# Attention and gated feed-forward on one core: the low parts of split q and k made on GpSimd, half of q split three steps sooner, and q of the last pairs loaded and rotated sooner

## The chip, the cores and the metric

The kernel runs on one core of a Trainium2 chip, as one program with five engines that run side by side: TensorE (PE in the rows; PEld is its weight load), VectorE (DVE), ScalarE (ACT), GpSimd (POOL) and SyncE (SP, which here only issues DMAs). Each engine works through its own instructions in the order in which they were written, and waits on semaphores for the others. The metric is the device time of one execution in microseconds (us), lower is better.

## What is computed

```python
def rotate(x):                       # rotary embedding, x1 and x2 are halves of the head
    return concat([x1 * cos - x2 * sin, x1 * sin + x2 * cos])
q_rot, k_rot = rotate(q), rotate(k)  # q, k, v: 4 batches x 8 heads x 576 tokens x 64
scores = q_rot @ k_rot.T / sqrt(64)
attn = softmax(scores)
x = (attn @ v)                       # heads put side by side: 4 x 576 x 512
h = relu(x @ w_in)                   # 512 -> 1024
c = conv over 3 neighbouring tokens of h, weights conv_w
out = (h * sigmoid(c)) @ w_out       # 1024 -> 512
```

All arrays are float32.

## The kernel before, in words

Two heads are treated together, which gives 16 pairs, numbered 0 to 15. A pair takes five steps, so pair p owns steps 5p to 5p+4; below they are called step 0 to step 4 of the pair. In each step one block of 128 query rows (64 in step 4, both heads at once) meets all 576 keys of its head. A step runs through these stations: the scores on TensorE into the PSUM tile `sp` (`emit_S`), the negated row maximum `negm` on VectorE (L292), the exponential on ScalarE into `st` (L296), and one step later the transposition of `st` on TensorE (L397) into PSUM tiles `tp`, which ScalarE copies to `pt` (L221). In step 0 of the next pair the product with v runs (L477), into PSUM tiles `pm`. From step 26 on, TensorE fills the rest of each step with the feed-forward part: first matmul units (L546, 24 matmuls each, whose results VectorE convolves at L565 and L567, and gates at L576) and halves of the second matmul (L658, whose two partial sums ScalarE and VectorE put together in `oh`, L672 and L673).

For speed, pairs 11 to 15 (`SPLITS = 11`) use split operands: a float32 x is written as hi + lo, where hi is x rounded by a copy to the type fp32r and lo = x - hi. The scores are then three products: KH with QH, KH with the low part of q, the low part of k with QH (L339; L333 for the last 64 rows, whose q lies in `QD`). The high parts QH, KH and QD are made by ScalarE (L370, L377, L386), the low parts `qL`, `kL` and half of QD by VectorE (L366, L375, L384), all of them in step 4 of the pair before (QD's low part in step 0 of the pair itself).

The rotated q and k come from the raw loads `rq` and `rk` (four DMAs each, issued by SP at L152, one buffer each). GpSimd multiplies them by a table (L192, six instructions for a tile) and adds the halves (L195, three instructions). VectorE turns the sum into `QT` and `KT` (L257, L260). GpSimd also makes the low parts of the feed-forward activations: `xT` and `xm` at L502, `gm` and `gb` at L585, each after ScalarE has made the high part.

What runs when is set by a table: `at(n, rank, fn)` puts a piece of work into step n, and within a step the pieces are written in the order of their ranks. Every engine then keeps that order. So a rank decides behind which other work of its engine an instruction stands. The tiles of the pool `p2` have two buffers for each tag: `QT` and `qL` share the tag `qT`, `KT` and `kL` the tag `kT`.

For the pair p the plan of before is: load q and k in step 5p-10 (rank 19.6), rotate q in step 5p-8 and k in step 5p-7, transpose both in step 5p-5 (rank 0.45), split in step 5p-1.

## Time and profile before

| What | Value |
|---|---|
| time, median of 3 runs | 465.98 us (465.52 to 466.04) |
| profiled execution, its own time | 466.01 us |
| profiled execution, span from the first to the last instruction | 464.2 us |
| granted TensorE clock over the span | 1.0 of full speed (the 2.4 GHz level) |
| busy: TensorE, VectorE, ScalarE, GpSimd | 448.6, 361.1, 333.4, 276.1 us |

The span is the profiler's; 1.8 us of the execution's own time lie around it. A busy engine is one that executes an instruction. Matmuls are pipelined, so that the busy time of TensorE is no measure of how close it is to its peak; what counts below is when TensorE stands still, and for whom.

### The profile page before, as it was taken

How to read it: one execution, taken by the hardware profiler on the slowest of the kernel's cores; microseconds unless marked ns; L12 is line 12 of the kernel's file. 1: busy time of each engine (PE TensorE's matmuls, PEld its weight loads, DVE VectorE, ACT ScalarE, POOL GpSimd, SP SyncE). 2: the span in 40 equal slices, each digit the busy share in tenths (PEclk: the TensorE clock that was granted, in tenths of full speed). 3: DMA queues.
4: the chain of work that ended last, by engine and by line, in shares of the span. 5: the costliest groups of instructions: out<-in, count | busy, mean ns of one | idle time of the engine just before them, and what ended most of it. 6: DMA issues, size and time to landing. Idle time of an engine off the chain costs nothing.

```text
span 464.2 us, 12800 instructions
## 1 busy us (share of the span) xinstructions
PE 448.6 (97%) x4843; PEld 353.5 (76%) x4843; DVE 361.1 (78%) x670; ACT 333.4 (72%) x960; POOL 276.1 (59%) x403
## 2 busy tenths in 40 slices
PE   8799999999999999999999989899999999999997
PEld 7366666666656767788887969798897978999886
DVE  6788999969998988687697997977976648468911
ACT  2899999979897878778696868778796844245500
POOL 1765555767998896979687593929530234144510
PEclk9999999999999999999999999999999999999999
DMA  9978784743463316142252517143110000100011
GB/s 226 240 173 222 197 222 111 203 105 79 117 129 75 68 42 137 38 104 63 55 101 61 120 38 140 39 97 81 29 51 34 18 28 0 47 23 24 0 70 45
DMA packets 103633, 42.36 MB, mean 91 GB/s; under 512 B 94524, under 2 KB 97876, under 8 KB 103572
## 3 DMA queue, kind: packets, MB, share of 16 engines
q1 hardware_dynamic: 103120, 41.20, 36.9%
q8 instruction: 38, 0.62, 0.6%
q10 hardware_dynamic: 452, 0.35, 0.2%
q14 instruction: 23, 0.19, 0.1%
HBM read 36.74 MB, written 4.79 MB: 89 GB/s over the span
## 4 chain that ended last, share of the span: by engine, by line
PE 71%; ACT 14%; DVE 11%; POOL 2%; issue 1%; DVEq 0%; POOLq 0%; ACTq 0%
PE mt L638 11%; PE pm L477 10%; PE pm L658 8%; PE pm L546 8%; PE mt L546 7%; PE tp L397 6%; PE sp L284 6%; ACT st L296 5%; ACT pt L221 4%; PE pm L527 4%; PE sp L339 3%; PE sp L477 3%; DVE c L567 3%; DVE negm L292 2%; DVE c L576 1%
## 5 line engine op out<-in xcount | busy, mean ns | idle before, releaser
L292 DVE TENSOR_REDUCE negm<-sp 128x1 f32<-128x576 f32 x144 | 102.6, 749 | 19.5 <-PE sp L339 6.9
L296 ACT ACTIVATE st<-sp,negm 128x576 f32<-128x576 f32 x128 | 94.2, 745 | 19.6 <-DVE negm L292 19.0
L221 ACT ACTIVATE pt<-tp 128x512 f32<-128x512 f32 (+3 forms) x176 | 84.7, 535 | 5.6 <-PE tp L397 5.0
L567 DVE SCALAR_TENSOR_TENSOR c<-rr,cw,c 128x288 f32<-128x288 f32 x128 | 80.5, 629 | 4.2
L585 POOL TENSOR_TENSOR gm<-c,gm 128x288 fp32r<-128x288 f32 (+4 forms) x72 | 46.4, 650 | 48.9 <-ACT gm L584 47.5
L284 PE MATMUL sp<-kT,qT 64*128 64x288 f32 (+3 forms) x352 | 64.3, 470 | 0.3 <-ACT kT L221 0.3
L397 PEld LDWEIGHTS tp<-idf,st 64*128 64x128 f32 x1024 | 40.4, 138 | 15.0 <-ACT st L296 6.7
L477 PE MATMUL pm<-pt,vm 128*64 128x290 f32 x368 | 49.7, 411 | 0.4 <-ACT pt L221 0.4
L658 PE MATMUL pm<-wouth,gm 64*128 64x256 f32 x512 | 49.8, 284 | 0.0
L397 PE MATMUL tp<-idf,st 64*128 64x64 f32 x1024 | 45.9, 226 | 3.5 <-ACT st L296 3.2
L192 POOL TENSOR_TENSOR rq<-rq,tabt 128x192 f32<-128x192 f32 x60 | 39.9, 697 | 13.7 <-DMA rq<-q 13.7
L576 DVE SCALAR_TENSOR_TENSOR c<-c,rr 128x288 f32<-128x288 f32 x64 | 38.3, 619 | 10.3 <-ACT c L573 10.3
L192 POOL TENSOR_TENSOR rk<-rk,tabt 128x192 f32<-128x192 f32 x60 | 41.0, 716 | 2.5 <-DVE negm L292 2.5
L658 PEld LDWEIGHTS pm<-wouth,gm 64*128 64x128 f32 x512 | 42.2, 186 | 0.0
L565 DVE TENSOR_SCALAR c<-rr,cw 128x288 f32<-128x288 f32 x56 | 25.2, 450 | 19.3 <-ACT rr L557 18.3
L284 PEld LDWEIGHTS sp<-kT,qT 64*128 64x128 f32 (+1 forms) x352 | 27.8, 173 | 15.4 <-issue 6.0
L477 PEld LDWEIGHTS pm<-pt,vm 128*64 128x64 f32 x368 | 25.6, 136 | 17.7 <-ACT pt L221 1.0
L502 POOL TENSOR_TENSOR xT<-xn,xT 128x290 fp32r<-128x290 f32 x18 | 16.0, 893 | 36.3 <-ACT xT L498 36.3
L658 PE MATMUL pm<-woutl,gm 64*128 64x256 f32 x256 | 37.6, 278 | 0.0
L573 ACT ACTIVATE c<-c 128x288 f32<-128x288 f32 x64 | 28.6, 447 | 12.1 <-DVE c L567 12.1
L546 PE MATMUL pm<-xT,wh 128*128 128x290 f32 x176 | 37.0, 302 | 0.0
L527 PE MATMUL pm<-xr,wr 128*64 128x290 f32 x256 | 33.9, 412 | 0.0
(161 smaller groups left out, 1064.5 us busy)
## 6 DMA issues: line engine op xcount, KB each, us to landing
rq<-q SPq DMA_DIRECT2D x60, 144.0 KB
rk<-k SPq DMA_DIRECT2D x60, 144.0 KB
w<-moe_w_in SPq DMA_DIRECT2D x8, 512.0 KB
vm<-v SPq DMA_DIRECT2D x32, 128.0 KB
rb<-rd SPq DMA_DIRECT2D x16, 144.0 KB
out<-oh SPq DMA_DIRECT2D x18, 128.0 KB
rb<-rd SPq DMA_DIRECT2D x16, 128.0 KB
w<-moe_w_out SPq DMA_DIRECT2D x4, 512.0 KB
```

Source lines behind the costliest of these rows:

```text
L192: nc.gpsimd.tensor_tensor(out=y, in0=y, in1=tabt[:, a:a + 3], op=ALU.mult)
L221: nc.scalar.activation(out=out, in_=in_, func=AF.Copy, scale=1.0 if sc is None else sc)
L284: nc.tensor.matmul(out=out, lhsT=qt[64 * h:64 * h + 64, c], rhs=kt[64 * h:64 * h + 64, a:a + n], start=True, stop=True)
L292: reds.setdefault((p, s), []).append(lambda: nc.vector.tensor_reduce(out=nm, in_=sc, axis=AX.XY if len(sc.shape) == 3 else AX.X, op=ALU.ma ...
L296: lambda: nc.scalar.activation(out=dst, in_=sc, func=AF.Exp, bias=nm, scale=1.0, accum_out=sm)
L397: nc.tensor.transpose(ps[r][:, 64 * k:64 * k + 64], x[i], idf[i, i])
L477: nc.tensor.matmul(out=xp[64 * h:64 * h + 64, :], lhsT=vmain[p][:, h, i, :] if i < 4 else vrem[p % 2][:, h, :], rhs=pt[:, 2 * i + h if i < ...
L527: nc.tensor.matmul(out=ps[a:a + 64], lhsT=w[:, a:a + 64], rhs=x, start=start, stop=stop)
L546: nc.tensor.matmul(out=ps[:, 0:XW], lhsT=w, rhs=x_at(xs, e), start=(i == 0), stop=(i == n - 1))
L567: nc.vector.scalar_tensor_tensor(out=c, in0=r[:, j + e:j + e + HS], scalar=cw[:, 8 * e + f:8 * e + f + 1], in1=c, op0=ALU.mult, op1=ALU.add,)
L638: nc.tensor.matmul(out=ops[tt][:, 0:width], lhsT=g_tile(tt, f, e), rhs=w[:, f, cols], start=(f == 0 and i == 0), stop=(f == NF - 1 and i = ...
L658: nc.tensor.matmul(out=ps[r][:, 0:256], lhsT=g_tile(tt, f, e)[rows], rhs=w[rows, f, cols], start=(f == 0 and i == 0), stop=(f == NF - 1 an ...
```

## The change

The low parts of q, k and QD move from VectorE to GpSimd (`lower`). They are kept in one tile each for all pairs (`late["qT"]`, `late["kT"]`, named `qTl` and `kTl`), which hold one of the two buffers of their tag for good. Rows 0 to 255 of q of pairs 12 to 15 are split in step 5p-4 in place of step 5p-1. In step 5p-1 KH comes first (rank 0.05) and the second half of QH and QD come behind the exponential (ranks 1.55 and 1.57); the low part of QD moves from step 5p to step 5p-1. For pairs 12 to 15 the load of q is issued right behind the transposition that frees its buffer (rank 0.46 in place of 19.6), its rotation moves from step 5p-8 to 5p-9, the multiplications of k from step 5p-7 to 5p-8, and the additions of k to step 5p-6 (rank 1.53).

```diff
-    def rope(p, part):
+    def rope(p, part, mult=True, add=True):
         x = raw[p, part]
-        for a in range(0, 18, 3):
+        for a in range(0, 18 * mult, 3):
             y = x[:, a:a + 3]
             nc.gpsimd.tensor_tensor(out=y, in0=y, in1=tabt[:, a:a + 3], op=ALU.mult)
-        for a in range(0, 18, 6):
+        for a in range(0, 18 * add, 6):
...
-            qs = (QD[:, 0], QD[:, 1]) if whole else (late["QH"][:, c], QL[p][:, c])
-            for i, (w, x) in enumerate(((qs[0], KH), (qs[1], KH), (qs[0], KL[p]))):
+            qs = (QD[:, 0], QD[:, 1]) if whole else (late["QH"][:, c], late["qT"][:, c])
+            for i, (w, x) in enumerate(((qs[0], KH), (qs[1], KH), (qs[0], late["kT"]))):
...
-    def split_q(p, low):
-        x = QT[p][:, 0:512]
+    def lower(tag, width, a, b, x, hi):
+        if tag not in late:
+            late[tag] = p2.tile([128, width], F32R, tag=tag, name=tag + "l")
+        nc.gpsimd.tensor_tensor(out=late[tag][:, a:b], in0=x, in1=hi.bitcast(F32), op=ALU.subtract)
+
+    def split_q(p, low, a, b):
+        x = QT[p][:, a:b]
         if low:
-            QL[p] = p2.tile([128, S], F32R, tag="qT", name="qL")
-            nc.vector.tensor_tensor(out=QL[p][:, 0:512], in0=x, in1=late["QH"].bitcast(F32), op=ALU.subtract)
+            lower("qT", S, a, b, x, late["QH"][:, a:b])
             return
...
-        nc.scalar.activation(out=late["QH"], in_=x, func=AF.Copy)
+        nc.scalar.activation(out=late["QH"][:, a:b], in_=x, func=AF.Copy)
 
     def split_k(p, low):
         if low:
-            KL[p] = p2.tile([128, S + 64], F32R, tag="kT", name="kL")
-            nc.vector.tensor_tensor(out=KL[p], in0=KT[p], in1=KH.bitcast(F32), op=ALU.subtract)
+            lower("kT", S + 64, 0, S + 64, KT[p], KH)
...
-                nc.vector.tensor_tensor(out=lo, in0=x, in1=hi.bitcast(F32), op=ALU.subtract)
+                nc.gpsimd.tensor_tensor(out=lo, in0=x, in1=hi.bitcast(F32), op=ALU.subtract)
...
-                        at(max(n - 10, WIDE) if early else n - 9 + 2 * i, 19.6 if early else 16 if p == 2 else 0.36, lambda p=p, part=part: load(p, part))
+                        at(max(n - 10, WIDE) if early else n - 9 + 2 * i, 0.46 if p > SPLITS and not i else 19.6 if early else 16 if p == 2 else 0.36, lambda p=p, part=part: load(p, part))
...
+                    elif p > SPLITS:
+                        at(n - 9 + i, 18, lambda p=p, part=part, i=i: rope(p, part, add=not i))
+                        if i:
+                            at(n - 6, 1.53, lambda p=p, part=part: rope(p, part, mult=False))
...
-                    for m, rank, fn, low in (
-                        (n - 1, 0.05, split_q, 0), (n - 1, 0.22, split_q, 1), (n - 1, 1.4, split_k, 0), (n - 1, 1.45, split_k, 1),
-                        (n - 1, 1.42, split_rest, 0), (n, 0.42, split_rest, 1),
+                    lead = (n - 4, 1.55) if p > SPLITS else (n - 1, 0.04)
+                    for (m, rank), fn in (
+                        (lead, lambda p, low: split_q(p, low, 0, 256)),
+                        ((n - 1, 0.05), split_k),
+                        ((n - 1, 1.55), lambda p, low: split_q(p, low, 256, 512)),
+                        ((n - 1, 1.57), split_rest),
                     ):
-                        at(m, rank, lambda fn=fn, p=p, low=low: fn(p, low))
+                        for low in range(2):
+                            at(m, 18.5 if low and m < n - 1 else rank + 0.05 * low, lambda fn=fn, p=p, low=low: fn(p, low))
```

On TensorE the order stays as it was. On GpSimd the stretch from the activations `gm` in step 1 of pair 12 to the next pair's `gm` in step 1 stood like this before (q and k are those of pair 14, which is rotated two pairs ahead).

```order
L502 TENSOR_TENSOR xT<-xn,xT 128x290
L192 TENSOR_TENSOR rq<-rq,tabt 128x192 x6
L195 TENSOR_TENSOR rq<-rq 128x6x32 x3
L502 TENSOR_TENSOR xT<-xn,xT 128x290
L192 TENSOR_TENSOR rk<-rk,tabt 128x192 x6
L195 TENSOR_TENSOR rk<-rk 128x6x32 x3
L585 TENSOR_TENSOR gm<-c,gm 128x288 x4
```

In the changed kernel the same stretch stands like this.

```order
L192 TENSOR_TENSOR rq<-rq,tabt 128x192 x6
L195 TENSOR_TENSOR rq<-rq 128x6x32 x3
L363 TENSOR_TENSOR qTl<-qT,QH 128x256
L503 TENSOR_TENSOR xT<-xn,xT 128x290
L192 TENSOR_TENSOR rk<-rk,tabt 128x192 x6
L503 TENSOR_TENSOR xT<-xn,xT 128x290
L363 TENSOR_TENSOR kTl<-kT,KH 128x640
L586 TENSOR_TENSOR gm<-c,gm 128x288 x2
L195 TENSOR_TENSOR rk<-rk 128x6x32 x3
L363 TENSOR_TENSOR qTl<-qT,QH 128x256
L385 TENSOR_TENSOR QD<-qT,QD 64x64 x2
L586 TENSOR_TENSOR gm<-c,gm 128x288 x2
```

The low part of k of pair 13 now stands behind both rotations' multiplications and both `xT`, and the additions of k, the second half of q and QD stand between the two groups of `gm`.

On VectorE, from step 4 of pair 12 to the transposition in step 0 of pair 13, the order before was this.

```order
L292 TENSOR_REDUCE negm<-sp 128x1
L366 TENSOR_TENSOR qL<-qT,QH 128x512
L565 TENSOR_SCALAR c<-rr_1576,cw 128x288
L567 SCALAR_TENSOR_TENSOR c<-rr_1576,cw,c 128x288 x2
L375 TENSOR_TENSOR kL<-kT,KH 128x640
L673 TENSOR_TENSOR oh<-oh,pm 128x256
L292 TENSOR_REDUCE negm<-sp 128x1 x2
L576 SCALAR_TENSOR_TENSOR c<-c,rr_1575 128x288
L576 SCALAR_TENSOR_TENSOR c<-c,rr_1576 128x288
L384 TENSOR_TENSOR QD<-qT,QD 64x64 x2
L257 STREAM_TRANSPOSE qT<-rq 128x576
```

In the changed kernel it is this.

```order
L292 TENSOR_REDUCE negm<-sp 128x1
L566 TENSOR_SCALAR c<-rr_1576,cw 128x288
L568 SCALAR_TENSOR_TENSOR c<-rr_1576,cw,c 128x288 x2
L674 TENSOR_TENSOR oh<-oh,pm 128x256
L292 TENSOR_REDUCE negm<-sp 128x1 x2
L577 SCALAR_TENSOR_TENSOR c<-c,rr_1575 128x288
L577 SCALAR_TENSOR_TENSOR c<-c,rr_1576 128x288
L257 STREAM_TRANSPOSE qT<-rq 128x576
```

Three kinds of subtraction have left VectorE; nothing else changed place there. The transposition of q (L257) writes the buffer that the low part of QD (L385, now on GpSimd) reads last.

On SP, the DMAs of step 0 of a pair stood like this before.

```order
L451 DMA rd<-rt 9x32 x4
L457 DMA rb<-rd 64x576
L458 DMA rb<-rd 64x512
L459 DMA rb<-rd 64x64
L152 DMA rq<-q 32x18x64 x4
L152 DMA rk<-k 32x18x64 x4
```

In the changed kernel they stand like this.

```order
L152 DMA rq<-q 32x18x64 x4
L452 DMA rd<-rt 9x32 x4
L458 DMA rb<-rd 64x576
L459 DMA rb<-rd 64x512
L460 DMA rb<-rd 64x64
L152 DMA rk<-k 32x18x64 x4
```

The four loads of q moved ahead of the round trip of the softmax denominators through DRAM (`rd`, `rb`).

## Rows read from the trace of the kernel before

**Rows 1.** The page, busy time, share of the span and instructions of each engine
```profile
PE 448.6 (97%) x4843; PEld 353.5 (76%) x4843; DVE 361.1 (78%) x670; ACT 333.4 (72%) x960; POOL 276.1 (59%) x403
```

**Rows 2.** Chain that ended last, 264 to 300 us: start, length, what
```profile
269.27 1.22 DVE kL L375
...
270.53 0.53 PE sp L339 x4
...
271.37 5.03 PE pm L477 x40
```

**Rows 3.** Timeline of TensorE: start, length, operation, count [idle before, releaser]
```profile
242.79 0.43 PE L339 MATMUL sp<-KH,qL 64*128 64x288 f32 x4
244.08 0.54 PE L339 MATMUL sp<-kL,QH 64*128 64x288 f32 x4 [0.86 <-DVE kL L375]
...
268.78 0.43 PE L339 MATMUL sp<-KH,qL 64*128 64x288 f32 x4
270.53 0.53 PE L339 MATMUL sp<-kL,QH 64*128 64x288 f32 x4 [1.31 <-DVE kL L375]
...
295.18 0.43 PE L339 MATMUL sp<-KH,qL 64*128 64x288 f32 x4
296.95 0.53 PE L339 MATMUL sp<-kL,QH 64*128 64x288 f32 x4 [1.33 <-DVE kL L375]
...
322.06 0.42 PE L339 MATMUL sp<-KH,qL 64*128 64x288 f32 x4
322.33 0.42 PE L339 MATMUL sp<-kL,QH 64*128 64x288 f32 x4
```

**Rows 4.** Timeline of GpSimd
```profile
226.98 0.67 POOL L585 TENSOR_TENSOR gm<-c,gm 128x224 fp32r<-128x224 f32 x1
...
235.03 2.15 POOL L192 TENSOR_TENSOR rq<-rq,tabt 128x192 f32<-128x192 f32 x3 [0.41 <-DMA rq<-q]
...
287.42 4.10 POOL L192 TENSOR_TENSOR rq<-rq,tabt 128x192 f32<-128x192 f32 x6
291.47 2.37 POOL L195 TENSOR_TENSOR rq<-rq 128x192 f32<-128x192 f32 x3
293.81 0.87 POOL L502 TENSOR_TENSOR xT<-xn,xT 128x290 fp32r<-128x290 f32 x1
294.64 4.37 POOL L192 TENSOR_TENSOR rk<-rk,tabt 128x192 f32<-128x192 f32 x6
298.97 2.12 POOL L195 TENSOR_TENSOR rk<-rk 128x192 f32<-128x192 f32 x3
301.05 1.57 POOL L585 TENSOR_TENSOR gm<-c,gm 128x288 fp32r<-128x288 f32 x2
```

**Rows 5.** GpSimd groups kept apart by shape: busy us, mean ns | idle before
```profile
L213 POOL TENSOR_TENSOR rq<-rq 128x576 f32<-128x576 f32 x5 | 7.2, 1431 | 5.9 <-DVE rvc L444 5.8
...
L777 POOL TENSOR_TENSOR woutl<-wf,wouth 128x256 fp32r<-128x256 f32 x8 | 6.3, 795 | 1.3 <-DVE wt L699 1.3
...
L585 POOL TENSOR_TENSOR gb<-c,gb 128x64 fp32r<-128x64 f32 x16 | 6.1, 382 | 0.1
```

**Rows 6.** Timeline of SP's DMA issues
```profile
230.00 2.15 SPq L152 DMA_DIRECT2D rq<-q  x4
...
307.64 3.36 SPq L152 DMA_DIRECT2D rq<-q  x4
```

**Rows 7.** Timeline of VectorE
```profile
220.77 0.77 DVE L257 STREAM_TRANSPOSE qT<-rq 128x576 f32<-128x576 f32 x1
...
280.33 0.37 DVE L565 TENSOR_SCALAR c<-rr,cw 128x288 f32<-128x288 f32 x1 [1.47 <-ACT rr L557]
280.73 1.07 DVE L567 SCALAR_TENSOR_TENSOR c<-rr,cw,c 128x288 f32<-128x288 f32 x2
...
290.31 1.51 DVE L567 SCALAR_TENSOR_TENSOR c<-rr,cw,c 128x288 f32<-128x288 f32 x2
```

**Rows 8.** Timeline of ScalarE
```profile
295.63 0.39 ACT L672 ACTIVATE oh<-pm 128x256 f32<-128x256 f32 x1
```

More of the change, by code (lines that the diff above doesn't have):

```diff
@@ L358, in emit_S @@
             soft(ps[:, :, 0:HS], st, 4)
-    QL, KL = {}, {}
-    def split_q(p, low):
-        x = QT[p][:, 0:512]
+    def lower(tag, width, a, b, x, hi):
[4 more added lines that the diff above has]
+        x = QT[p][:, a:b]
         if low:
-            QL[p] = p2.tile([128, S], F32R, tag="qT", name="qL")
-            nc.vector.tensor_tensor(out=QL[p][:, 0:512], in0=x, in1=late["QH"].bitcast(F32), op=ALU.subtract)
+            lower("qT", S, a, b, x, late["QH"][:, a:b])
             return
```

## The prediction, made before the changed kernel ran

> **What bounds the kernel now.** I read the page first: TensorE is busy for 97% of the span [rows 1], so only its idle time can be won without taking matmuls away, and the change takes none away. The waits of TensorE between 240 and 365 us, where the split pairs lie, name a single cause: VectorE's low part of k. The chain that ended last shows how it comes about: kL on VectorE at 269.27, then the third product on TensorE at 270.53 [rows 2]. The timeline of TensorE then gives the sizes. In step 0 of pairs 11, 12 and 13 the product with kL starts after 0.86, 1.31 and 1.33 us of idle; in pair 14 it follows the second product by 0.27 us (322.06 to 322.33) with no idle [rows 3], and pair 15 looks like pair 14. Measured from where it could have started, 0.27 us behind the second product, the third comes 1.02 us late in pair 11 (244.08 against 243.06), 1.48 in pair 12 and 1.50 in pair 13 [rows 3]. So 4.0 us is what removing this wait can give at most, and TensorE's own pace between two such products is 24.97 us (244.08 to 268.78 + 0.27), then 24.92 and 25.38 [rows 3].
>
> **What the change removes.** VectorE loses qL, kL and QD's low part. Its order then has the convolution directly before `oh`, and TensorE no longer waits for VectorE at this place. That is worth the 4.0 us only if GpSimd delivers the low part of k in time.
>
> **What it adds to GpSimd.** The trace has no such subtraction there, but has the same kind of instruction in other widths: 256 columns take 0.80 us and 576 take 1.43 on average [rows 5]. From these two, 640 columns (kTl) come to 1.56 us. A half of qTl is 0.80. For QD's two pieces I take two instructions of 64 columns, 2 x 0.38 = 0.76 [rows 5]. Each pair thus adds 3.9 us to GpSimd. It is idle enough for the sum, so the question is where kTl stands in its order: behind both rotations' multiplications and both `xT`.
>
> **A closed loop.** With `qTl` holding one of the two buffers for good, q of the next pair can be transposed only after GpSimd has made QD's low part; only then is the next load of q issued; the rotation waits for that load; and kTl stands behind the rotation. So one kTl depends on the one before it. Its length, piece by piece:
> - from one kTl: the first two `gm` 1.57 [rows 4], the additions of k (in the 13.63 below), half of qTl 0.80, QD 0.76;
> - the transposition of q 0.77 [rows 7];
> - the load of q. The one row that shows a load's end: issued at 230.00 [rows 6], used at 235.03 after GpSimd had waited 0.41 us for it [rows 4], 5.0 us, with the loads of k right behind it. In the changed kernel small transfers follow instead, so I take 4.7. The bounds are 2.15 (the issue alone) and 6.2 (5.0 plus the 1.2 by which one issue took longer, 3.36 against 2.15 [rows 6]);
> - rotation of q, one `xT`, rotation of k: from 287.42 to 301.05, 13.63 us [rows 4]. Second `xT` 0.87, other half of qTl 0.80, kTl 1.56.
>
> Sum: 1.57 + 0.80 + 0.76 + 0.77 + 4.7 + 13.63 + 0.87 + 0.80 + 1.56 = 25.5 us (25.8 from pair 11 to 12, where four smaller instructions stand in place of the two `gm`: 2 x (0.67 + 0.38) against 1.57 [rows 4, 5], which I put at 0.3, since their starts overlap). This is 0.5 above TensorE's own pace and 0.9 below the 26.4 us that now pass from 244.08 to 270.53 and from there to 296.95 [rows 3].
>
> **The first kTl.** The transposition for pair 11 ends at 221.54 [rows 7]; with the earlier load the rotation of pair 12's q can start once GpSimd is free, at 227.65 [rows 4], in place of 235.03. Rotation of q 6.39 (287.42 to 293.81), `xm` 0.83 give 234.9. The load of k takes the place of that of q at 230.00, so it is there at 235.0. Multiplications of k 4.33, `xm` 0.83, half of qTl 0.80, kTl 1.56 end at 242.5 [rows 4, 5]. TensorE needs it at 243.06: no wait, 1.0 us won.
>
> **Going round.** Pair 12: kTl at 242.5 + 25.8 = 268.3, needed at 243.06 + 24.97 = 268.0; it starts at 268.3, 2.2 before the 270.53 of now. Pair 13: 268.3 + 25.5 = 293.8, needed at 293.2; 3.1 before 296.95. Pair 14: 319.3, needed at 319.2; 3.0 before 322.33. Pair 15 has no rotation in the loop, and all that follows starts earlier by the same 3.0 us.
>
> **What else is queued behind the new waits.** The transposition on VectorE now waits for QD on GpSimd; behind it stand kT's transposition, the reciprocals and `negm` of step 1. By the sum above it starts about as late in absolute time as now while TensorE has come forward, so this `negm` loses its reserve. On ScalarE the first half of QH is added in step 1 and half of QH is gone from step 4. TensorE's product with v needs the tiles that ScalarE's `oh` (ends 296.02 [rows 8]) and one copy behind it empty; without the kL wait TensorE reaches it 0.84 us after the third product (270.53 to 271.37 [rows 2]), at 295.45 + 0.84 = 296.3. The reserve is under 0.3 us. For such edges I charge 0.15 us in each of three pairs, 0.5 in all; the bounds are nothing and 0.44 a pair, by which two convolution instructions get longer beside GpSimd (1.51 against 1.07 [rows 7]). The moved loads of q cost SP 2.15 us ahead of `rd` and `rb`, which are used two steps later; that costs nothing unless `rb` comes more than a step late.
>
> **A rule weighed against the trace.** GpSimd's earlier rotation falls into steps 1 and 2, where it stood idle. VectorE's two convolution instructions took 1.07 us there and 1.51 beside a rotation, the scaling 0.37 [rows 7]; eight such instructions by 0.22 make 1.8 us a pair at most, against 1.47 of idle time that VectorE spends in step 1 waiting for ScalarE [rows 7]. The Trainium skill, SBUF — State Buffer, § Who interferes with whom, says that a VectorE instruction with two SBUF inputs and a GpSimd instruction that reads SBUF exclude each other, and that the loser is blocked for the whole of the other. By that rule each of the eight could wait for a rotation instruction to end; the price of it stands with the fourth rival. The trace bears out that they get longer, by less than a whole instruction.
>
> **The rivals.**
> - The loop is shorter than TensorE's pace (chance 0.12). For it: rotations elsewhere run faster, and the load may land sooner than 4.7. With 24.9 or less no wait is left, 4.0 us are won: 462.0.
> - The loop is 26.2 to 26.7 us (0.13): a load at its upper bound or slower rotations. In pair 14 the product then starts at 242.8 + 3 x 26.4 = 322.0, as now; with 26.2 and 26.7 it is 465.1 and 466.6, no change.
> - ScalarE's edge in step 0 costs 0.5 us a pair and more (0.10): about 1.5 us are won, 464.5.
> - The other side (0.10): in step 2 VectorE falls so far behind that the exponentials of step 3 hold up TensorE. A rotation instruction is 4.10 / 6 = 0.68 us [rows 4]; if each of the eight instructions waits for half of one, VectorE is 2.7 us late, 1.25 above its 1.47 of idle time, in each of three pairs: 3.75 us lost against 3.0 won, 466.8; if each waits for three quarters of one, 4.1 us, it is 7.9 against 3.0, 470.9. It decides from 2.5 us a pair, where loss and gain are equal. Against it: the row above shows 0.22 an instruction.
>
> **How the numbers follow.** The profiled execution's own time is 466.01, 0.03 above the median. My forecast (0.55): 466.01 - 3.0 + 0.5 = 463.5; its own range is 462.3 to 464.8 (a loop between 25.0 and 26.0). What a measurement can tell from no change is about 0.2%, 0.93 us. Faster is the forecast, the first and the third rival, 0.77; same 0.13; slower 0.10. The range runs from 461.8, just beyond the 4.0 us, to 466.0, which leaves out the fourth rival and half of the second.
>
> **What would show it.** Right: the third product in step 0 of pairs 12 and 13 waits under 0.7 us, now for GpSimd; kTl starts about 25.5 us apart; the rotation of q starts about 6 us after the end of the transposition or sooner; pair 15 starts 2.5 to 3 us earlier. Wrong: kTl more than 26.4 us apart, waits of TensorE for ScalarE in steps 2 to 3, or a VectorE that waits for GpSimd at the transposition until `negm` of step 1 is late by over 1 us.

## The result, and the profile after

The changed kernel took 469.56 us (median of 8 runs, 466.84 to 471.46), the kernel before 466.27 (8 runs, 465.52 to 466.97): ratio 1.0069, 95% interval 1.0040 to 1.0097. It is slower, where 463.5 was forecast. The profiled execution of the changed kernel took 471.46 us with a span of 469.5, so the median's losses are 1.9 us smaller than those read from its trace. Helper lines are one higher than before (L566 is the scaling that was L565).

The page shows GpSimd busier by 16 us than [rows 1], and TensorE at 96% of a longer span:

```profile
PE 452.1 (96%) x4843; PEld 354.9 (76%) x4843; DVE 361.3 (77%) x650; ACT 333.6 (71%) x965; POOL 292.1 (62%) x428
```

The timeline of TensorE, where [rows 3] had the three waits for kL:

```profile
236.85 1.57 PE L284 MATMUL sp<-kT,qT 64*128 64x288 f32 x4 [2.50 <-ACT st L296]
...
249.02 0.43 PE L339 MATMUL sp<-KH,qTl 64*128 64x288 f32 x4
249.29 0.43 PE L339 MATMUL sp<-kTl,QH 64*128 64x288 f32 x4
...
267.00 0.27 PE L436 MATMUL pm<-idf,st 64*128 64x64 f32 x1 [0.63 <-ACT pt L221]
...
275.20 0.43 PE L339 MATMUL sp<-KH,qTl 64*128 64x288 f32 x4
275.46 0.43 PE L339 MATMUL sp<-kTl,QH 64*128 64x288 f32 x4
...
292.94 0.28 PE L436 MATMUL pm<-idf,st 64*128 64x64 f32 x1 [0.63 <-ACT pt L221]
...
318.35 0.64 PE L436 MATMUL pm<-idf,st 64*128 64x64 f32 x2 [0.43 <-ACT pt L221]
```

The third product now follows the second by 0.27 and 0.26 us: the wait is gone. New are a wait of 2.50 us in pair 10, ahead of all that the split concerns, and waits in step 3 of pairs 11 to 13. The same instructions of TensorE in both traces give the balance (starts in us; "gate" and "gate, xn" are the kernels e9 and e10 below):

```
                                     before   after         gate    gate, xn
24 us, code that is unchanged         23.85   +1.21        +0.89     -0.56
end of step 1, pair 10               232.73   +1.35        +1.47     -0.61
step 3 of pair 10                    235.39   +6.23        +3.03     +1.09
third product, pair 11               244.08   +5.21        +2.02     +0.07
step 3 of pair 11                    261.29   +6.43        +3.18     +0.60
third product, pair 12               270.53   +4.93        +1.70     -0.89
step 3 of pair 12                    287.71   +5.94        +2.44     -0.57
third product, pair 13               296.95   +4.45        +0.95     -1.11
step 3 of pair 13                    313.75   +5.25        +1.83     -0.58
last matmul                          460.66   +5.27        +1.85     -0.52
```

After wins 1.02, 1.50 and 1.49 us at the third products, 4.0 in all; it loses 1.22, 1.01 and 0.80 in steps 2 to 3 of the pairs between, 3.0 in all, and 4.9 us at once in step 2 of pair 10. The 1.2 at 24 us arise in code that the change leaves as it was. VectorE's scaling of `wt`, a weight tile, took 2.77 us in after, behind a run of 18 instructions of GpSimd that ended at 20.43, and 0.67 us in before. TensorE waits 1.72 us, until 21.33, for a copy of VectorE behind it. VectorE before, then VectorE and GpSimd after:

```profile
18.59 0.67 DVE L688 TENSOR_SCALAR wt<-wt 128x512 f32<-128x512 f32 x1
```

```profile
17.95 2.77 DVE L689 TENSOR_SCALAR wt<-wt 128x512 f32<-128x512 f32 x1
```

```profile
18.74 1.69 POOL L195 TENSOR_TENSOR rk<-rk 128x192 f32<-128x192 f32 x3
```

The 0.9 of "gate" came about without that (its scaling took 0.56 us), and "gate, xn" has no such loss.

VectorE and GpSimd at the large loss:

```profile
226.25 0.35 DVE L445 SCALAR_TENSOR_TENSOR rvc<-sums 128x9 f32<-128x9 f32 x1
...
227.01 1.38 DVE L292 TENSOR_REDUCE negm<-sp 128x1 f32<-128x576 f32 x2
229.73 4.43 DVE L566 TENSOR_SCALAR c<-rr,cw 128x288 f32<-128x288 f32 x1 [1.33 <-ACT rr L558]
234.19 0.52 DVE L568 SCALAR_TENSOR_TENSOR c<-rr,cw,c 128x288 f32<-128x288 f32 x1
```

```profile
228.06 0.32 POOL L586 TENSOR_TENSOR gb<-c,gb 128x64 fp32r<-128x64 f32 x1
228.33 0.67 POOL L586 TENSOR_TENSOR gm<-c,gm 128x224 fp32r<-128x224 f32 x1
228.97 3.36 POOL L192 TENSOR_TENSOR rq<-rq,tabt 128x192 f32<-128x192 f32 x6
232.28 1.72 POOL L195 TENSOR_TENSOR rq<-rq 128x192 f32<-128x192 f32 x3
```

A scaling that takes 0.37 us [rows 7] took 4.43: it was released during the second product of pair 12's rotation and ended at 234.16, 0.16 us after the last sum (234.00). The rotation stands there because its load was moved; before, GpSimd began it at 235.03 [rows 4]. Behind the scaling, the convolution and the maxima came late, so the exponentials, so TensorE. The windows show TensorE's wait and the granted clock:

```profile
234.00:236.00 2.00, 0.35 (x6) 0.14 (x3) 1.93 (x5) 0.47 (x2) 0.00 (x0) 1.00 0.61 107
236.00:238.00 2.00, 1.15 (x4) 0.72 (x6) 1.93 (x5) 2.00 (x6) 0.00 (x0) 0.80 0.00 0
238.00:241.00 3.00, 3.00 (x26) 2.25 (x25) 2.92 (x6) 2.96 (x11) 1.82 (x3) 0.57 0.16 49
```

(Stretch, length, busy time and count of PE, PEld, DVE, ACT and POOL, granted clock, DMA share, GB/s.) TensorE idles, then runs at half the clock, 1.2 in place of 2.4 GHz, for some 3.4 us. The clock is the smaller part of the 4.9 us. In e13 and e14 (below) the same scaling is blocked for 4.61 and 4.69 us, TensorE waits 2.69 and 2.76 us, and the granted clock stays at 1.00; step 2 of pair 10 still loses 4.1 and 4.2 us there. So about 0.8 of the 4.9 us is left for the clock in this execution. TensorE and the windows in e13:

```profile
235.27 1.71 PE L287 MATMUL sp<-kT,qT 64*128 64x288 f32 x7 [2.69 <-ACT st L299]
```

```profile
236.00:238.00 2.00, 2.00 (x25) 1.52 (x24) 1.92 (x5) 1.96 (x7) 0.40 (x1) 1.00 0.03 8
238.00:241.00 3.00, 3.00 (x22) 2.93 (x23) 2.53 (x5) 2.94 (x9) 3.00 (x5) 1.00 0.17 49
```

In step 2 of pair 12 VectorE's order is the same as before, and the pieces are longer beside the moved rotation: the two convolution instructions take 1.51 us (289.11) in place of 1.07, the two `xn` 1.76 in place of 0.83. VectorE before, then after:

```profile
285.13 0.83 DVE L495 TENSOR_TENSOR xn<-xn,rb 128x290 f32<-128x290 f32 x2
```

```profile
290.55 1.76 DVE L496 TENSOR_TENSOR xn<-xn,rb 128x290 f32<-128x290 f32 x2
292.22 0.41 DVE L674 TENSOR_TENSOR oh<-oh,pm 128x256 f32<-128x256 f32 x1
```

`oh` ends at 292.63, ScalarE's copy out of the same tiles follows, and TensorE's transposition waits for that until 292.94.

### The profile page after: what moved, and what is told of

Read it like the earlier page. It is cut to its first block, busy times and chain, and to the rows that moved or that the text cites. A ratio compares the mean times of both kernels' runs of the same rounds, so it can differ in the third digit from the quotient of the medians.

```text
span 469.5 us, 12787 instructions
## 1 busy us (share of the span) xinstructions
PE 452.1 (96%) x4843; PEld 354.9 (76%) x4843; DVE 361.3 (77%) x650; ACT 333.6 (71%) x965; POOL 292.1 (62%) x428
## 4 chain that ended last, share of the span: by engine, by line
PE 73%; ACT 10%; DVE 7%; POOL 7%; issue 1%; DMA 1%; POOLq 0%; DVEq 0%; ACTq 0%
PE mt L639 11%; PE pm L478 10%; PE pm L659 9%; PE pm L547 8%; PE sp L284 7%; PE mt L547 7%; PE tp L398 7%; PE pm L528 4%; ACT st L296 3%; PE sp L339 3%; ACT pt L221 3%; PE sp L478 3%; POOL rq L192 2%; POOL rk L192 2%; POOL wlo L524 1%
## 5 line engine op out<-in xcount | busy, mean ns | idle before, releaser
L568 DVE SCALAR_TENSOR_TENSOR c<-rr,cw,c 128x288 f32<-128x288 f32 x128 | 84.4, 659 | 4.2
L284 PE MATMUL sp<-kT,qT 64*128 64x288 f32 (+3 forms) x352 | 67.0, 482 | 2.6 <-ACT st L296 2.5
L398 PEld LDWEIGHTS tp<-idf,st 64*128 64x128 f32 x1024 | 41.6, 141 | 15.7 <-ACT st L296 5.4
L398 PE MATMUL tp<-idf,st 64*128 64x64 f32 x1024 | 47.2, 229 | 4.1 <-ACT st L296 2.2
L566 DVE TENSOR_SCALAR c<-rr,cw 128x288 f32<-128x288 f32 x56 | 31.5, 563 | 25.2 <-ACT rr L558 25.0
L192 POOL TENSOR_TENSOR rq<-rq,tabt 128x192 f32<-128x192 f32 x60 | 38.9, 681 | 17.3 <-DVE wt L700 9.3
L577 DVE SCALAR_TENSOR_TENSOR c<-c,rr 128x288 f32<-128x288 f32 x64 | 38.3, 619 | 10.3 <-ACT c L574 10.3
L284 PEld LDWEIGHTS sp<-kT,qT 64*128 64x128 f32 (+1 forms) x352 | 28.8, 177 | 19.3 <-issue 7.2
L192 POOL TENSOR_TENSOR rk<-rk,tabt 128x192 f32<-128x192 f32 x60 | 39.7, 696 | 1.9 <-DVE negm L292 1.9
L547 PEld LDWEIGHTS pm<-xT,wh 128*128 128x128 f32 x176 | 28.2, 189 | 0.5
```

What stands on the lines that cost most here:

```text
L192: nc.gpsimd.tensor_tensor(out=y, in0=y, in1=tabt[:, a:a + 3], op=ALU.mult)
L284: nc.tensor.matmul(out=out, lhsT=qt[64 * h:64 * h + 64, c], rhs=kt[64 * h:64 * h + 64, a:a + n], start=True, stop=True)
L398: nc.tensor.transpose(ps[r][:, 64 * k:64 * k + 64], x[i], idf[i, i])
L547: nc.tensor.matmul(out=ps[:, 0:XW], lhsT=w, rhs=x_at(xs, e), start=(i == 0), stop=(i == n - 1))
L568: nc.vector.scalar_tensor_tensor(out=c, in0=r[:, j + e:j + e + HS], scalar=cw[:, 8 * e + f:8 * e + f + 1], in1=c, op0=ALU.mult, op1=ALU.add,)
```

## The experiments

**e1 and e2: each half of the change alone.** e1 is the changed kernel with loads and rotations as before, e2 the kernel before with loads and rotations moved. The cuts of code from here on show only the parts of lines that differ:

```diff
-    0.46 if p > SPLITS and not i else 19.6 if early
+    19.6 if early                                     # e1
-    elif p > SPLITS:
+    elif p > NP:                                      # e1
```

> Low parts on GpSimd and the first half of q split three steps sooner, but all loads and rotations where they were before. In GpSimd's order kTl then stands behind the additions of k. In the trace of before, the first xT of a pair (286.65, 16.1 us after the third product of step 0) to the end of those additions takes 14.4 us, kTl 1.6 more: 32 us after the last kTl-fed product, needed after 24.9. All theories: TensorE waits some 7 us for GpSimd in step 0 of pairs 11 to 14, so 475 to 490 us. Blocking theory (the earlier rotation of pair 12 is what met VectorE's scaling in step 51): no scaling of over 1.5 us there and times within 1 us of each other. Clock theory (dips come by themselves): the times still spread by 3 us or more and the granted clock falls without a long VectorE instruction ahead of it.

> Loads and rotations of pairs 12 to 15 moved as in the change, low parts on VectorE as before. Blocking theory: TensorE still waits for kL in step 0 of pairs 11 to 13 (3 to 4 us in all), and now also in step 3 of pairs 11 to 13 behind VectorE's late oh (1.5 to 3 us in all), and a scaling of over 2 us in step 51 in some executions, which costs up to 5: 467 to 473 us, times spread by 2 us or more. Low-part theory (qTl and kTl on GpSimd lengthen VectorE's step 2, not the rotation): no wait in step 3, about 466.

e1: 494.38 us (494.08 to 496.03), ratio 1.0608 (1.0591 to 1.0626), above the 475 to 490 that all theories had. e2: 472.51 (472.02 to 474.77), 1.0129 (1.0114 to 1.0144), within the range of the blocking theory. Without the moves the low parts stand behind the rotations; the timeline of TensorE in e1 and the window around it:

```profile
248.46 0.85 PE L339 MATMUL sp<-KH,qTl 64*128 64x288 f32 x4 [5.34 <-POOL qTl L363]
249.95 0.85 PE L339 MATMUL sp<-kTl,QH 64*128 64x288 f32 x4 [0.65 <-POOL kTl L363]
```

```profile
247.00:250.00 3.00, 0.89 (x6) 0.55 (x6) 0.00 (x0) 0.00 (x0) 3.00 (x5) 0.50 0.23 52
```

Four products take 0.85 us at clock 0.50, against 0.43 in after. So the moves are needed; but e2 shows that they bring the loss by themselves, the same scaling included, with every low part still on VectorE:

```profile
228.09 4.43 DVE L565 TENSOR_SCALAR c<-rr,cw 128x288 f32<-128x288 f32 x1 [1.33 <-ACT rr L557]
```

**e3: pair 12 as before** (`p > SPLITS + 1` in both places), the rest changed.

> The changed kernel, but pair 12 is loaded and rotated where it was before; pairs 13 to 15 stay moved. Blocking theory: the scaling in step 51 meets no chain of rotation instructions, so no instruction of 4 us there and no clock dip behind it; the profile's 5 us between 232 and 240 us are gone; what stays is 4.0 won at kL less up to 3.0 lost in step 3 of pairs 11 to 13, plus a wait in step 0 of pair 11, where kTl again stands behind pair 12's late rotation (rotation from 235, kTl at 250, needed at 243: some 6 us). So 468 to 472 with a spread under 1.5 us. Clock theory: the spread stays at 3 us or more, with dips at any place.

473.79 us (473.21 to 474.91), 1.0163 (1.0147 to 1.0179), above the expected range. The scaling is not blocked (0.37 us), but TensorE waits 5.33 us for qTl of pair 11, which stands behind pair 12's rotations as in e1. It tells nothing on the price of the scaling: it brought in another loss.

**e4: the other way to the same end**, the kernel before with kL ahead of the convolution on VectorE (`split_k` at 0.06 and 0.24).

> The kernel before with one edit: KH and kL of the next pair go ahead of the convolution in step 4 (ranks 0.06 and 0.24 in place of 1.4 and 1.45). All stays on VectorE, GpSimd is left alone. If the wait for kL is only a matter of VectorE's order, kL ends some 1.2 us before TensorE needs it, the three waits vanish and 3.5 to 4.0 us are won: 462.0 to 462.8. Rival: the convolution, now behind kL, makes oh late and TensorE waits for the tiles pm in step 0 instead: 464 to 466.

466.5 us (464.32 to 467.89, 12 runs), 1.0001 (0.9987 to 1.0016), above both ranges. The kL waits are gone: the third product of pair 13 is 2.83 us earlier than before in the trace. All of it is lost in the same pair, where ScalarE's `oh` waits for the store of the half before it, which shares its one buffer:

```profile
317.20 0.38 ACT L672 ACTIVATE oh<-pm 128x256 f32<-128x256 f32 x1 [2.65 <-DMA out<-oh]
```

The profiled execution is the slowest of the twelve. Two of the others took 464.32 and 464.65 us; whether the store came in time there is not known.

**e5, e6, e7: the form of the scaling, and VectorE's order.**

```diff
+    if blk and late["n"] in (51, 52):                 # e5, e7
+        nc.vector.scalar_tensor_tensor(
+            out=c, in0=r[:, j:j + HS], scalar=cw[:, f:f + 1], in1=zero[:, 0:1].to_broadcast([128, HS]),
+            op0=ALU.mult, op1=ALU.add,
+        )
-    1.7 + j                                           # the rank of norms
+    3.1 + 0.1 * j if p > 9 else 1.7 + j               # e6, e7
```

> The changed kernel; the two convolutions that are written out in steps 51 and 52 make their first product with a scalar_tensor_tensor (the scaling plus a zero that is read as a second operand) and not with a tensor_scalar, and nothing else differs. Blocking theory (the tensor_scalar of 4.43 us, which stood behind eight of GpSimd's instructions, cost the 5 us around 230 to 241 us, the stretch at half clock behind it included): no instruction of VectorE over 1 us there but the reductions, no wait of TensorE of 2.5 us, granted clock 0.9 or more from 232 to 242 us, 464.5 to 466.8 us. Clock theory (TensorE's clock falls there by itself): the fall and the wait stay, 469 to 470 us. If the form does not matter, the new instruction takes 4 us in its turn: 469 to 470 us.

> The changed kernel; the two normalisations (xn) of pairs 10 and later stand behind the sum of the output half (oh) on VectorE in step 2, not one ahead of it and one between. Blocking theory (in steps 2 of pairs 11 to 13 the moved rotation and the low part of q lengthen VectorE's chain ahead of oh, and TensorE's transposition of step 3 waits for it): the waits of TensorE's line L436 on ScalarE's pt at 266, 293 and 318 us (0.2 to 0.9 us each, with what follows 3.0 us) are under 0.2 us, 466.3 to 467.8 us, a wait at 237 us staying where the scaling is blocked. Low-part theory (GpSimd's own new work is what is late, and TensorE would wait for it as soon as VectorE is not in the way): the third product of step 0 waits for kTl, which now stands behind both low parts of x, 469 to 471 us.

> Both edits, that of the scaling's form and that of the normalisations. Blocking theory: the whole 4.0 us of the old waits for kL is kept, and little of it is given back: 461.5 to 464.0 us, faster than either kernel. Clock theory: 468 to 470 us. Low-part theory: 466 to 468 us.

e5: 474.58 us, 1.0161 (1.0139 to 1.0183); e6: 472.35, 1.0120 (1.0089 to 1.0151); e7: 474.84, 1.0148 (1.0112 to 1.0183). All three miss the ranges of the blocking theory. In e5 the other form is blocked just as long:

```profile
229.75 4.58 DVE L567 SCALAR_TENSOR_TENSOR c<-rr,cw,zero 128x288 f32<-128x288 f32 x1 [1.34 <-ACT rr L559]
```

The Trainium skill, SBUF — State Buffer, § Who interferes with whom, says that a VectorE instruction with two inputs in SBUF contends with GpSimd's reads too; the row agrees, and e5 was a poor test for that reason. In e6 the step-3 waits fell from 2.5 to 0.7 us between 200 and 330, but kTl came too late behind both low parts of x, and TensorE waited for it in pair 13. The group of TensorE:

```profile
L339 PE MATMUL sp<-kTl,QH 64*128 64x288 f32 x52 | 5.8, 299 | 1.5 <-POOL kTl L363 1.5
```

**e9, e10, e12: the rotation gated.** The first product of pair 12's rotation waits for the scaling; e10 also puts the second `xn` of pairs 10 and later behind `oh`, e12 both of pair 9 as well.

```diff
+    if p == SPLITS + 1 and part == "q" and not a:     # in rope()
+        late["v"] = late["w"]                         # the scaling
+        gated(ins)
-    1.7 + j                                           # the rank of norms
+    3.1 if j and p > 9 else 1.7 + j                   # e10
+    3.1 + 0.1 * j if p == 9 or j and p > 9 else 1.7 + j   # e12
```

> The changed kernel; the first product of the rotation of pair 12's q waits for the scaling of the first of the two convolutions of steps 51 and 52 (the one that took 4.43 us behind the rotation), so that the rotation starts behind it, about 0.9 us later than it did. Blocking theory: that scaling takes 0.37 us, TensorE does not wait 2.5 us at 237 us, and the clock does not fall behind it: of the 5 us lost there 4 or more come back, 463.5 to 466.0 us. Clock theory: the clock falls there whatever VectorE does, 468 to 470 us. If the rotation only blocks the second convolution (scaling about 1.4 us later) in the same way: 4 us there instead, 468 to 471 us.

> The same gate, and the second normalisation (xn) of pairs 10 and later behind the sum of the output half (oh) in step 2; GpSimd's order and ScalarE's stay. Blocking theory: VectorE reaches oh about 0.9 us sooner in steps 2 of pairs 11 to 13, the waits of TensorE's line of the transposition on ScalarE's pt (0.2 to 0.7 us at 266, 293 and 318 us) vanish and the low part of k is not later: 2 to 3 us less than the kernel with the gate alone, 461.5 to 463.5 us if the gate itself does what it should. Low-part theory: the wait moves to the third product of step 0 (kTl): within 0.5 us of the kernel with the gate alone.

> The changed kernel with the gate, the second normalisation of pairs 10 and later behind the sum oh, and of pair 9 both. Blocking theory: the two waits in step 3 of pair 10 (0.95 and 0.73 us in the kernel with the gate and one normalisation moved) shrink to under 0.5 us together, 464.3 to 465.8 us, under the kernel before. If VectorE is not what sets that edge: 466.0 to 466.5 us, as with the gate and one normalisation.

e9: 467.70 us (466.62 to 468.37, 12 runs), 1.0024 (1.0011 to 1.0037). e10: 466.18 (465.48 to 466.62, 12 runs), 0.9993 (0.9985 to 1.0002). e12: 466.07 (465.11 to 467.57, 12 runs), 0.9985 (0.9972 to 0.9998). All three are slower than the blocking theory had them. VectorE and GpSimd in e9:

```profile
229.74 0.37 DVE L569 TENSOR_SCALAR c<-rr,cw 128x288 f32<-128x288 f32 x1 [1.33 <-ACT rr L561]
```

```profile
230.19 3.87 POOL L192 TENSOR_TENSOR rq<-rq,tabt 128x192 f32<-128x192 f32 x6 [0.95 <-DVE c L569]
```

The scaling is back at 0.37 and the granted clock from 234 to 241 us at 1.00. By the table above the loss in step 2 of pair 10 falls from 4.9 to 1.6 us. e10 takes the edges of pairs 11 to 13 down from 2.8 in e9 (1.16, 0.74, 0.88) to 1.4 (0.53, 0.32, 0.53), half of what was expected. But what the third product gives falls with them, 1.02, 1.49 and 0.54: TensorE now comes sooner than GpSimd. TensorE and GpSimd in pair 13 of e10:

```profile
295.84 0.53 PE L342 MATMUL sp<-kTl,QH 64*128 64x288 f32 x4 [0.79 <-POOL kTl L366]
```

```profile
289.13 3.95 POOL L192 TENSOR_TENSOR rk<-rk,tabt 128x192 f32<-128x192 f32 x6 [0.77 <-DMA rk<-k]
```

In e10's trace 3.05 us won at the third products stand against 1.70 lost in pair 10 and 1.38 at the edges. In e12, whose profiled execution is the slowest of its twelve, the next thing is late, the transfer of `rb`, whose small loads now follow the moved loads of q. VectorE, then SP:

```profile
260.89 0.84 DVE L499 TENSOR_TENSOR xn<-xn,rb 128x290 f32<-128x290 f32 x1 [0.49 <-DMA rb<-rd]
```

```profile
251.74 1.03 SPq L152 DMA_DIRECT2D rq<-q  x2
252.87 1.43 SPq L455 DMA_DIRECT2D rd<-rt  x4
256.00 0.46 SPq L461 DMA_DIRECT2D rb<-rd  x1
```

and TensorE waits 1.10 us at 262.38. e12 is the only version whose interval lies under the kernel before, by 0.15%, which is less than the 0.2% that a measurement here can tell from no change.

**e16: all repairs together**, both `xn` of pairs 9 and later behind `oh`, and the low parts of x of pairs 9 to 13 behind kTl.

> The changed kernel with the gate; both normalisations of pairs 9 and later behind the sum oh, and the low parts of x of pairs 9 to 13 two steps later, behind the low part of k on GpSimd. Blocking theory: neither the edge of step 3 nor the third product of step 0 waits over 0.3 us, 463.3 to 465.3 us, faster than the kernel before. If the low part of k is late for another reason (GpSimd's loop is full, as the first rival of the prediction has it), or the transfer of rb becomes the wait: 465.5 to 466.5 us.

468.43 us (468.12 to 470.27), 1.0049 (1.0029 to 1.0068), above both ranges. The third product waits no more, but TensorE then waits 0.18 to 0.27 us for ScalarE's copies at nine places between 244 and 320 us; why ScalarE is late there stays open.

**e8, e11, e15: the blocking by itself.** GpSimd runs the nine instructions of `rope`, VectorE arrives with one. The core of e8, with the delay first:

```
b = nc.scalar.activation(out=r[:, 0:32 + 24 * n], in_=ps[:, 0:32 + 24 * n], func=AF.Copy)
...
d = nc.vector.tensor_scalar(out=c, in0=r[:, 0:288], scalar1=cw, scalar2=None, op0=ALU.mult)
wait(d, b)
```

> This kernel leaves the whole computation out: 84 times GpSimd runs the nine instructions of one rotation (six products of 128x192, three sums of 128x192) back to back while VectorE, idle until then, is released by ScalarE for one instruction of 128x288 at a point that moves by about 17 ns from one time to the next; the first 42 times it is the tensor_scalar, the last 42 the scalar_tensor_tensor. Blocking theory in its narrow form (the loser waits out the instruction of GpSimd that runs, and only at some points of arrival several of them): most of the first 42 take 0.37 to 0.85 us, a few, arriving about 0.2 us behind the start of a product, over 3 us; none of the last 42 over 1 us. In its broad form (a tensor_scalar waits for the whole chain): nearly all of the first 42 over 3 us. If the 4.43 us came from something else at that place of the kernel: none of the 84 over 1 us.

> This kernel leaves the whole computation out: 112 times GpSimd runs eight subtractions like the low parts of the gates (64 and 224 columns) and then the nine instructions of a rotation, 17 without a pause, while VectorE takes four maxima from PSUM, goes idle, and is released by ScalarE for one tensor_scalar of 128x288 within the first products of the rotation, about 5 ns later each time. Blocking theory: where it arrives 0.200 to 0.213 us behind the start of a product (as the five blocked scalings so far), it waits out all that is left of the rotation, over 3 us; elsewhere 0.37 to 0.85 us. If the blocked scalings need more than a long run of GpSimd and that point of arrival (the kernel's TensorE, transfers or addresses): none of the 112 over 1 us.

> This kernel leaves the whole computation out: 90 times the run of 17 instructions of GpSimd, and one tensor_scalar of VectorE that arrives within the second and third product of the rotation, 30 ns later each time, in five groups of 18: the scaling also waits on GpSimd's own semaphore, long met (group 1); four loads like that of k run beside it (2); TensorE runs 48 products beside it (3); VectorE transposes first, as in the kernel (4); all four (5). If one of these is what makes the scaling of step 51 wait out the rotation, the groups that have it show 2.5 to 4.5 us, the others 0.37 to 0.9. If none shows over 1 us, the cause is none of them, and stays open.

The scaling took 0.37 to 0.80 us in e8 (42 times), 0.37 to 0.88 in e11 (112) and 0.37 to 0.87 in e15 (90, all five groups alike); the form with two tensors 0.52 to 0.94 (e8, 42). Its length follows from the point of arrival: 0.71 us when it comes 0.04 behind the start of a product, 0.39 at 0.365, 0.37 to 0.485, and from 0.505 on 0.80 (e8). So it waits for the end of the instruction that runs, or, when it comes just ahead of that end, of the next one. None waited for a whole rotation. So the point of arrival, loads, TensorE, transpositions and a second semaphore do not make one by themselves behind a short run of GpSimd.

**e13, e14: the point of arrival in the kernel.** One more product of 16 or 64 columns on GpSimd ahead of the rotation shifts it.

> The changed kernel with one more instruction of GpSimd, a product of 128x16 on a tile of its own, ahead of the rotation of pair 12's q, which so starts about 0.2 us later; order and waits of everything else stay. Point-of-arrival theory: the scaling at 229.7 us no longer arrives 0.20 us behind the start of a product, and takes 0.37 to 0.9 us; 465 to 468 us. Place theory (something else at that place makes a scaling that meets the rotation wait it out): 3.5 to 4.6 us again, 469 to 471 us.

> The same with a product of 128x64, so that the rotation starts about 0.3 us later. Point-of-arrival theory: the scaling takes 0.37 to 0.9 us, 465 to 468 us. Place theory: 3.5 to 4.7 us, 469 to 471 us.

e13: 470.7 us, 1.0084 (1.0060 to 1.0108); e14: 472.5, 1.0127 (1.0104 to 1.0151). The scaling is blocked at both points (4.61 and 4.69 us), so the point of arrival is not the cause in the kernel either. e14 is slower than either theory had it: its profiled execution took 469.64 us at a granted clock of 1.0, its other four 471.75 to 472.90 at 0.989 to 0.993. VectorE in e13, where the scaling came 0.03 us behind the start of a product:

```profile
227.96 4.61 DVE L569 TENSOR_SCALAR c<-rr,cw 128x288 f32<-128x288 f32 x1 [1.33 <-ACT rr L561]
```

**e17, e18: the run of GpSimd ahead of it.** All blocked scalings of the convolution met GpSimd late in a run of instructions without a pause; in after it was the 38th since 208.66 us. Earlier in the same run VectorE was let in, last for its two gates (L577) at the 20th and 22nd; the blocked scaling met the 15th that began after these had ended at 222.19. Transpositions, maxima and instructions of 9 columns lie between. e17 is the kernel of e15 without the groups' additions, with a run that grows from group to group and a release of VectorE that moves with it.

```diff
-    for e in range(4):                  # pairs of subtractions ahead of the rotation
+    for e in range(4 + 4 * group):      # e17
```

> This kernel leaves the whole computation out: the scaling against one rotation again, 70 times in five groups of 14, with 8, 16, 24, 32 and 40 subtractions of GpSimd ahead of the rotation without a pause, since in the traces of the whole kernel the blocked scalings met GpSimd after 37 or 38 instructions without a pause. If the length of GpSimd's run decides: the later groups show 2.5 to 4.7 us, the first 0.37 to 0.9. If it does not: all 0.37 to 0.95 us, and what makes the place stays open.

> This kernel leaves the whole computation out: the scaling against one rotation, 60 times in six groups of 10, with other runs of GpSimd ahead of the rotation: 10, 12 and 14 subtractions of 64 and 224 columns (groups 1 to 3, 4.5 to 6.3 us), 18 of 64 columns (group 4, about 5 us), 6 and 10 of 576 columns (groups 5 and 6, about 8 and 14 us). If it is the number of GpSimd's instructions without a pause that decides (blocked from somewhere between the 12th and the 19th on): group 4 is blocked to the end of the run (over 1.5 us), groups 5 and 6 are not (under 0.95), and groups 1 to 3 show from which number on. If it is the length of the run in time (between 4.8 and 8.5 us): group 4 is not blocked, groups 5 and 6 are.

In e17 the length of the run ahead is enough to block the scaling. Each row is 14 trials:

```
subtractions ahead   scaling meets GpSimd's    it lasts, us
 8                   10th to 12th              0.37 to 0.86
16                   19th to 20th              3.02 to 3.54
24                   29th to 30th              2.19 to 2.70
32                   38th to 39th              1.35 to 1.88
40                   48th to 49th              0.50 to 1.03
```

VectorE and GpSimd, a trial of the second row:

```profile
300.92 3.10 DVE L113 TENSOR_SCALAR c<-rr,cw 128x288 f32<-128x288 f32 x1 [6.07 <-ACT rr L64]
```

```profile
291.76 7.17 POOL L70 TENSOR_TENSOR gm<-d,gm 128x64 f32<-128x64 f32 x16 [1.67 <-ACT go L58]
298.90 3.31 POOL L76 TENSOR_TENSOR rq<-rq,tabt 128x192 f32<-128x192 f32 x6
302.18 1.66 POOL L79 TENSOR_TENSOR rq<-rq 128x192 f32<-128x192 f32 x3
```

It ends at 304.02, 0.18 us after the run (303.84), as the one of the kernel did. Later arrivals wait less, since less of the run is left. e18 did not tell number from time: each of its subtractions waited for the one before, which left 78 ns between them, and with these pauses none of 60 scalings took over 0.81 us, not even after 14 us of such work. That is an answer of another kind: the run must be without pauses. How long VectorE had been idle does not decide: 1.33 us ahead of the blocked scaling of after, 5.6 to 19.4 ahead of those of e17, up to 13.7 ahead of scalings of e18 that were not blocked.

## Why the prediction was wrong

**What held.** The wait for kL went, and gave the 4.0 us that [rows 3] set as its ceiling. kTl took 1.57 us (forecast 1.56). From one kTl to the next it was 25.9 us (246.16 to 272.08 to 298.02; forecast 25.8 and 25.5), but that agreement is luck: kTl waited there 0.23 and 0.25 us for ScalarE's KH, so that TensorE's own delay in steps 2 to 3 set the distance, and not the loop. Where TensorE is not so delayed (e10), the loop is 26.18 and 26.78 us (241.06 to 267.24 to 294.02), in the second rival's range or next to it, and TensorE waits 0.79 us in pair 13. The load of q was mis-sized: in e10 that of pair 14 was issued at 275.11 and used at 280.89, 5.8 us in place of 4.7. GpSimd in after, then SP and GpSimd in e10:

```profile
272.08 1.57 POOL L363 TENSOR_TENSOR kTl<-kT,KH 128x640 fp32r<-128x640 f32 x1 [0.23 <-ACT KH L378]
```

```profile
275.11 2.98 SPq L152 DMA_DIRECT2D rq<-q  x4
```

```profile
280.89 3.66 POOL L192 TENSOR_TENSOR rq<-rq,tabt 128x192 f32<-128x192 f32 x6 [2.96 <-DMA rq<-q]
```

**The step that failed: "The first kTl".** It started pair 12's rotation "once GpSimd is free, at 227.65", and asked only when GpSimd and the load allow it, not what VectorE does from there to 234. The scaling of step 51 met it and waited for all of it: 4.9 us were lost there, of which e9 gives 3.3 back; the other 1.6 stay with VectorE slowed beside the rotation (0.5 in e12, where both `xn` stand behind `oh`). This is near the fourth rival, at a place and a price that it did not have: one instruction of pair 10 that waits for a whole run, and not eight in each of three pairs that wait for a part of one instruction. The sentence that weighed the rule ("by less than a whole instruction") was right for its rows, and for e8, e11 and e15; its rows had only rotations that GpSimd began right behind a pause [rows 4], or one instruction later (the one at 287.42). On this the Trainium skill (SBUF — State Buffer, § Who interferes with whom) says that the loser is blocked until the other's instruction is finished. Short runs agree (0.94 us at most); a long run does not: 4.43 us behind eight instructions. The measurement decides. e9 shows that meeting the rotation is the cause: with the rotation 0.95 us later, the block, the wait of 2.50 us and the half clock are gone. The block does not always bring the half clock with it, as e13 and e14 show.

**A term mis-sized: the edges.** 0.5 us for three pairs was charged, 3.0 came (1.22, 1.01, 0.80), and at another place: not ScalarE's `oh` in step 0, but VectorE in step 2, where two `xn` (1.76 us) and the convolution, all longer beside the rotation, stand ahead of `oh`. These are the waits for ScalarE in steps 2 to 3 that the prediction named as a sign of being wrong, and they lie where the fourth rival put its loss, at 0.8 to 1.2 us a pair. e10 shows it for half of them: with one `xn` moved behind `oh`, and the order on GpSimd and ScalarE as in e9, the edges fall from 2.8 to 1.4. What makes the other half stays open.

**Two smaller errors.** The loads of q were costed at nothing ahead of `rd` and `rb`, "unless `rb` comes more than a step late"; in after that was so, in e12, where TensorE is sooner, `rb` is late by 0.49 us at 260.89. And the forecast took one wait out and let the rest stand: e4 removes the same wait without GpSimd, and its median comes out at 1.0001.

**The sum.** 1.2 (the start, in unchanged code, where the scaling of `wt` was blocked) + 4.9 + 3.0 - 4.0 = 5.1, against 5.27 at the last matmul of the profiled execution; the median is 3.3 slower. How often the scaling of step 51 is blocked in runs without a profile cannot be read; it was in all seven profiled kernels with the moved rotation and no gate. The mean clock of each run is on record: 0.993 to 0.996 in the four of 469.95 us and more, 0.999 at 469.15 and 469.18, 0.996 at 467.46 and 1.0 at 466.84. The blocked executions of e13 and e14 at a clock of 0.999 and 1.0 took 469.50 and 469.64 us. So the runs near 469 fit a blocked scaling without the half clock, and those near 467 one that was not blocked, or a quick start; that is argued, not shown.

## What to carry to other kernels

Before work is moved on GpSimd, look at VectorE's rows for the whole stretch that it will then cover, and see whether it joins what stands ahead of it to a run without pauses; one wait put into such a run costs GpSimd 0.95 us here and gave 1.9 back. A wait of TensorE that is removed is worth its length only if the next edge is further away than that: three ways of removing this one (e4, e10, e12) all ended within 0.2% of the kernel before. Put the instruction that frees a shared tile (`oh`) ahead of the ones that have time (`xn`).

## What the runs showed of the hardware that was not expected

- A VectorE instruction on SBUF waited for a whole run of GpSimd, up to 4.69 us (e14), when it came in late in a run without pauses: in e17 always from the 19th instruction on (56 trials). When it came at the 12th or sooner, it waited for the end of the instruction that ran, or of the next one (258 trials of the scaling, 0.88 us at most). In between both occur. The scaling of `wt` met the run of 18 instructions at the start at its 13th to 16th in seven profiled kernels, and was blocked in one (after, at the 14th, 2.77 us; before, at the 16th, 0.67 us). In e18, pauses of 78 ns ahead of the rotation were enough to keep it from being blocked. Whether number or time decides, and from which instruction the count starts, is open.
- The blocked engine's opponent was hardly slowed: a product took 0.59 to 0.61 us beside the blocked scaling, and 0.65 where the scaling came in between (e8).
- After a wait of 2.50 us in after, TensorE ran at half the clock for some 3.4 us; after waits of 2.69 (e13) and 2.76 us (e14) at the same place the granted clock stayed at 1.00. So the length of the wait alone does not tell whether the clock falls. After the waits of 0.86 to 1.33 us of [rows 3] the product behind took 0.53 to 0.54 us for its four, against 0.43.
